# A convolution and mixture-of-experts kernel: the third group's convolution in four pieces a half group on TensorE in place of five

## The chip, the cores and the metric

The kernel runs on one core of one Trainium2 chip. The metric is the device time of one execution in microseconds (us). The kernel before takes 1198.82 us, the median of three runs (1196.96 to 1201.81).

The engines are named as the profile names them: PE is TensorE (PEld its weight loads), DVE is VectorE, ACT is ScalarE, POOL is GpSimd, SP is SyncE, which issues most DMAs.

## The reference

The input `x` has 8 sequences of 2880 positions with 192 channels, so 23040 tokens. Two steps follow each other.

The first is a dynamic convolution: for each token and each of 8 heads, 7 weights come from a softmax over `weight_gen`, and the output is the weighted sum of the token and its 6 predecessors, head by head (24 channels each):

```python
out = np.einsum('bshk,bskhg->bshg', w, x_unf)
```

The second is a two-level mixture of experts. Each token picks the best of 4 groups by `x @ w_group`, then the best of 4 experts in it by `xg @ w_expert[g]`. The expert is `relu(x @ w1) @ w2` with 1024 hidden units, and its output is multiplied by both softmax values:

```python
h = np.maximum(xg[mask_e] @ w1[g, e], 0.0)
ye = h @ w2[g, e]
out[tok_idx] = combined[:, None] * ye
```

## The kernel before

**Groups and half groups.** The 23040 tokens lie on 128 partitions, 180 to a partition. They are worked on in 15 groups of 12 columns (1536 tokens), each in two half groups of 6 columns (`SC = 6`). For a group the kernel loads `xin` and `wt` (`load_group`, L124 and L134, SyncE), takes the softmax (`softmax`, L278 to L292, VectorE with one exponential on ScalarE), convolves (`conv`), scores the tokens against all groups and experts (`logits`: transposes L406 and L407, score matmuls L389, transposes back L433, all on TensorE, with copies L399, L413, L425, L436 on ScalarE), ranks them (`ranks`, L359 to L503, many small VectorE instructions) and scatters each row of tokens to its expert's region in DRAM (`scatter_row`, L516 and L517, GpSimd).

**Two ways to convolve.** A half group needs 7 products of 128 x 1152 elements (L307, VectorE) and their sum. In the first three groups, that is the half groups 0 to 5, TensorE adds: for each piece of a list, VectorE makes the products of the piece, adds those of one piece to each other (L343), and TensorE multiplies the piece by the identity and accumulates it in three banks (L348, three matmuls of 128 x 384 for each piece). After the last piece ScalarE copies the three banks to `xrow` (L351). From the fourth group on VectorE adds all by itself (L325). The lists stand in `SUMS`, one for each half group; `FIVE` is `((0, 1), (2, 3), (4,), (5,), (6,))`: two pairs and three single products, so five pieces, 15 matmuls and two adds. The products use three buffers `pr` in turn.

**Rounds and blocks.** After every group but the first a round of expert blocks can be filled. The first round (after two groups) has ten plain blocks of 128 tokens; the later ones have mostly blocks of 256. A block loads its tokens `xb` from DRAM (L818), its weights (L833 for the first layer of a plain block, L835 and L842 into `raw` for the others, L846 for the second layer), transposes the tokens (L915 for plain blocks, L926 and L927 for the others), and runs the first layer (L953), the relu on ScalarE (L959), the second layer (L991), the scaling by the gate (L1000) and the scatter to the output (L1008, GpSimd).

**What sets the order.** Each engine works through its own instruction list in order. The lists of TensorE, ScalarE, VectorE and SyncE are written out by a planner in the kernel: it keeps an estimated clock for each engine (`clk`, `run`), and `fill` lets the front part (softmax, convolution, scores, ranks) emit VectorE work until its clock reaches that of the expert matmuls. A block may be emitted when its round's tables are due (`arrive`). So a change of one list of pieces shifts the estimated clocks, and with them the places at which later instructions stand, until the order falls back into the old one. The lines that the change acts through, with `1.27` us as the planner's cost of a product or an add and `1.92` as that of a piece on TensorE:

```python
            pieces = sum_banks(CHUNK[g] + n)
            pattern = SUMS[CHUNK[g] + n]
            for j, ks in enumerate(pattern):
```

Of the kernel before, what the change touches and what calls it, by code (L numbers as in the profile page):

```python
# [30 lines left out]
TURNED = ((6, 5), (4,), (3,), (2,), (1,), (0,))  # L31
FOUR = ((0, 1, 2), (3, 4), (5, 6))
FIVE = ((0, 1), (2, 3), (4,), (5,), (6,))
HALF = ((0, 1), (2, 3), (4, 5), (6,))
SUMS = (TURNED, FIVE, FIVE, FIVE, FIVE, FIVE)


class Slot:
# [4 lines left out]
def conv_moe_kernel(ctx: ExitStack, tc: tile.TileContext, x, wgen, w_group, w_expert, w1, w2, out):  # L43
# [254 lines left out]
    def sum_banks(k):  # L298
        at = [(3 * k + i) % 4 for i in range(3)] if k < CHUNK[FIRST] else [2, 0, 1]
        return [banks[a]([P, 2, D]) for a in at]  # L300

    def conv(g, o):
# [3 lines left out]
        def product(c0, k, dst):  # L306
            nc.vector.tensor_tensor(  # L307
                out=dst, in0=o.xin[:, c0 + k:c0 + k + SC, :].rearrange("p s (h g) -> p s h g", g=HG),
                in1=w4[:, c0:c0 + SC, :, k:k + 1].broadcast_to([P, SC, H, HG]), op=ALU.mult)

        for n, c0 in enumerate(range(0, WIDTHS[g], SC)):
            row = o.xrow[n]
            acc = row[:, :, 0:D].rearrange("p s (h g) -> p s h g", g=HG)
            new = lambda: cv.tile([P, SC, H, HG], F32, name="pr", bufs=3)
            if state["slots"] or CHUNK[g] + n >= len(SUMS):
                product(c0, 0, acc)
# [13 lines left out]
# [3 lines that stand above are left out]
# [899 lines left out]
```

## Time and profile before

| What | Value |
|---|---|
| Median of three runs | 1198.82 us |
| Profiled execution | 1198.2 us |
| Its span | 1196.6 us |
| TensorE busy | 1125.1 us, 94% |
| VectorE busy | 955.8 us, 80% |
| ScalarE busy | 643.9 us, 54% |
| GpSimd busy | 583.6 us, 49% |
| DMA traffic | 275.10 MB, mean 230 GB/s |

The profiled execution is one run of the program; its span is the time from its first to its last instruction, and the run's own time is 1.6 us longer. An engine's busy share is an average over the whole span; the third group's convolution, which the change is about, lies in the stretch from about 75 to 120 us, in which the shares are other than on average. In the views, "idle before, releaser" is the time that the engine stood still ahead of a row, and what ended it; "issue" means that nothing which the profile shows was waited for. A matmul of 32-bit floats leaves two records.

### The profile page before, as it was taken

Reading aid. Unit: us, or ns where it says so; the run is one execution under the profiler, and the core shown is the slowest. Engines: PE = TensorE matmul, PEld = TensorE weight load, DVE = VectorE, ACT = ScalarE, POOL = GpSimd, SP = SyncE. Lnnn points to the kernel's source line nnn. Section 1 sums busy time; section 2 is a strip of 40 time slices with the busy share of each in tenths; the row PEclk is TensorE's granted clock in tenths of the full one; section 3 lists DMA queues with packets and bytes.
Section 4 is the critical chain, followed back from the end, with each engine's and each line's share of the span. In section 5 each row is a group of like instructions: output and inputs, shape, how many; then the busy total and the mean of one; then the engine's idle time right before and its main releaser. Section 6 shows DMA issues by size and latency. Waiting matters only on the chain.

```text
span 1196.6 us, 24607 instructions
## 1 busy us (share of the span) xinstructions
PE 1125.1 (94%) x8357; PEld 1062.7 (89%) x8357; DVE 955.8 (80%) x1682; ACT 643.9 (54%) x1235; POOL 583.6 (49%) x613
## 2 busy tenths in 40 slices
PE   5887999999999999999999999999799899999998
PEld 2444888999999999999989999999699899999997
DVE  8899997989998989998988889898374576655661
ACT  1332435555555555565546556565446676555762
POOL 7164284647274745765564738384636312222211
PEclk9898999999999999999999999999999999999999
DMA  5797999887878877778786868767657875655562
GB/s 172 216 312 227 298 310 286 247 272 229 286 233 255 256 249 235 248 246 281 221 284 197 289 202 281 232 181 227 201 154 235 263 241 154 189 174 179 161 200 76
DMA packets 84521, 275.10 MB, mean 230 GB/s; under 512 B 15491, under 2 KB 34379, under 8 KB 82593
## 3 DMA queue, kind: packets, MB, share of 16 engines
q1 hardware_dynamic: 64056, 229.77, 61.3%
q0 software_dynamic: 20208, 43.39, 11.9%
q8 instruction: 67, 1.10, 0.4%
q14 instruction: 70, 0.57, 0.1%
q10 hardware_dynamic: 120, 0.28, 0.1%
HBM read 225.83 MB, written 48.42 MB: 229 GB/s over the span
## 4 chain that ended last, share of the span: by engine, by line
PE 62%; issue 19%; DVE 6%; POOL 4%; ACT 3%; DMA 3%; another core or an unknown queue 2%; POOLq 1%; SPq 0%; DVEq 0%; ACTq 0%
PE py L991 27%; PE ph L953 25%; POOL out L1008 4%; DVE pr L307 2%; PE pl L389 2%; PE ph L348 1%; PE tpx L927 1%; PE tpx L926 1%; DMA xb<-rows 1%; PE tpx L348 1%; PE tp L406 1%; DMA rows<-rem 1%; PE py L348 1%; PE pl L406 1%
## 5 line engine op out<-in xcount | busy, mean ns | idle before, releaser
L953 PE MATMUL ph<-xh,wa 128*128 128x256 f32 (+3 forms) x1992 | 455.5, 303 | 1.2 <-issue 1.1
L1008 POOL DMA_INDIRECT out<-y,xb x189 | 213.9, 1132 | 425.6 <-ACT y L1000 176.7
L991 PE MATMUL py<-wc,hh 128*128 128x192 f32 x2160 | 401.3, 327 | 2.7 <-ACT y L1000 2.2
L953 PE MATMUL ph<-xl,wa 128*128 128x256 f32 (+3 forms) x1328 | 351.9, 286 | 0.3
L991 PEld LDWEIGHTS py<-wc,hh 128*128 128x128 f32 x2160 | 346.0, 190 | 4.7 <-ACT y L1000 2.8
L953 PEld LDWEIGHTS ph<-xh,wa 128*128 128x128 f32 x1992 | 337.7, 190 | 4.2 <-issue 2.1
L959 ACT ACTIVATE hh<-ph 128x512 f32<-128x512 f32 (+2 forms) x296 | 165.9, 561 | 265.9 <-PE ph L953 239.0
L953 PEld LDWEIGHTS ph<-xl,wa 128*128 128x128 f32 x1328 | 252.1, 190 | 1.1 <-issue 0.8
L307 DVE TENSOR_TENSOR pr<-xin,wt 128x1152 f32<-128x1152 f32 x186 | 249.3, 1351 | 4.7 <-PE py L348 3.4
L517 POOL DMA_INDIRECT rows<-xrow,ix x156 | 222.2, 1424 | 45.6 <-POOL ix L516 31.5
L325 DVE TENSOR_TENSOR xrow<-xrow,pr 128x1152 f32<-128x1152 f32 x144 | 194.9, 1353 | 0.7
L883 DVE SCALAR_TENSOR_TENSOR pr<-ph,hh 128x320 fp32r<-128x320 f32 (+2 forms) x128 | 71.7, 560 | 92.5 <-ACT hh L964 85.6
L883 DVE TENSOR_TENSOR wa<-raw,wa 128x1024 fp32r<-128x1024 f32 x83 | 101.3, 1220 | 31.9 <-ACT wa L859 30.7
L516 POOL COPY ix<-posi 128x1 int32<-128x1 int32 x156 | 76.0, 499 | 79.1 <-DMA rows<-xrow,ix 44.7
L993 PE MATMUL py<-wc,hh 128*128 128x384 f32 x352 | 111.6, 364 | 0.0
L964 ACT ACTIVATE hh<-ph 128x320 fp32r<-128x320 f32 (+2 forms) x128 | 63.8, 499 | 72.0 <-PE ph L953 71.1
L994 PE MATMUL py<-wc,pr 128*128 128x192 f32 x352 | 88.5, 251 | 0.0
L859 ACT CAST wa<-raw 128x1024 fp32r<-128x1024 f32 x83 | 87.1, 1050 | 0.0
L868 ACT CAST wa<-raw 128x1024 fp32r<-128x1024 f32 x83 | 86.8, 1046 | 0.0
L1000 ACT ACTIVATE y<-py,xb 128x192 f32<-128x192 f32 x179 | 67.3, 423 | 20.9 <-PE py L991 16.7
L883 DVE TENSOR_TENSOR xl<-tpx,xh 128x512 fp32r<-128x512 f32 (+1 forms) x92 | 59.3, 644 | 11.4 <-ACT xh L933 10.4
L993 PEld LDWEIGHTS py<-wc,hh 128*128 128x128 f32 x352 | 66.5, 189 | 1.3
(194 smaller groups left out, 1355.4 us busy)
## 6 DMA issues: line engine op xcount, KB each, us to landing
wc<-in_moe_w SPq DMA_DIRECT2D x73, 768.0 KB
raw<-in_moe_w SPq DMA_DIRECT2D x83, 512.0 KB
xin<-in_x SPq DMA_DIRECT2D x14, 1728.0 KB
raw<-in_moe_w SPq DMA_DIRECT2D x91, 256.0 KB
raw<-w1lo SPq DMA_DIRECT2D x83, 256.0 KB
raw<-in_moe_w SPq DMA_DIRECT2D x22, 768.0 KB
xb<-rows SPq DMA_DIRECT2D x75, 194.0 KB
wa<-in_moe_w SPq DMA_DIRECT2D x24, 384.0 KB
```

The lines of the kernel that those rows point to most:

```text
L307: nc.vector.tensor_tensor(out=dst, in0=o.xin[:, c0 + k:c0 + k + SC, :].rearrange("p s (h g) -> p s h g", g=HG), in1=w4[:, c0:c0 + SC, :, k ...
L325: nc.vector.tensor_tensor(out=acc, in0=acc, in1=prs[k - 2], op=ALU.add)
L517: written_once(nc.gpsimd.indirect_dma_start(out=rows[:, :], out_offset=bass.IndirectOffsetOnAxis(ap=ix, axis=0), in_=src, in_offset=None, ...
L859: nc.scalar.copy(out=o.wa[:, 0, :], in_=o.raw[0])
L868: nc.scalar.copy(out=o.wa[:, 2, :], in_=o.raw[1])
L883: f(*a, **k)
L953: nc.tensor.matmul(ph[:, v, :], lhsT=w[:, f0:f0 + P], rhs=rhs, start=i == 0, stop=i == len(terms) - 1)
L959: nc.scalar.activation(out=hh, in_=ph, func=AF.Relu)
L991: nc.tensor.matmul(b.acc[t], lhsT=hh[:, v, c], rhs=wc[0][:, f, :], start=f == 0 and not (b.wide and t == 1), stop=f == NFT - 1 and not (b. ...
L993: nc.tensor.matmul(b.py[t], lhsT=hh[:, v, c], rhs=wc[f // 4][:, f % 4].rearrange("p l d -> p (l d)"), start=f == 0, stop=False)
L994: nc.tensor.matmul(b.acc[t], lhsT=hl[:, v, c], rhs=wc[f // 4][:, f % 4, 0, :], start=False, stop=f == NFT - 1)
L1008: ins = nc.gpsimd.indirect_dma_start(out=out[:, :], out_offset=bass.IndirectOffsetOnAxis(ap=b.x.bitcast(I32)[:, t, D + 1:D + 2], axis=0), ...
```

## The change

The half groups 4 and 5, the third group's, take the list `HALF`, which stood in the file without being used:

```diff
 FIVE = ((0, 1), (2, 3), (4,), (5,), (6,))
 HALF = ((0, 1), (2, 3), (4, 5), (6,))
-SUMS = (TURNED, FIVE, FIVE, FIVE, FIVE, FIVE)
+SUMS = (TURNED, FIVE, FIVE, FIVE, HALF, HALF)
```

In each of the two, VectorE adds the products 4 and 5 (one more L343) and TensorE takes them as one piece (three L348 fewer). So 87 L348 matmuls are left of 93, and 13 L343 adds stand where 11 stood. The planner's order moves with it on every engine, up to some 350 us into the program.

VectorE, at the end of half group 4: `pr` are the product buffers, `wt`, `m` and `z` belong to the softmax of the fourth group, which is emitted in between.

```order
 L280 TENSOR_TENSOR wt<-wt,m 128x672
+L343 TENSOR_TENSOR pr<-pr 128x1152
 L307 TENSOR_TENSOR pr<-xin,wt 128x1152
 L286 TENSOR_REDUCE z<-wt 128x96
 L288 TENSOR_SCALAR z<-z 128x96
 L290 RECIPROCAL z<-z 128x96
-L307 TENSOR_TENSOR pr<-xin,wt 128x1152
 L292 TENSOR_TENSOR wt<-wt,z 128x672
-L307 TENSOR_TENSOR pr<-xin,wt 128x1152
+L307 TENSOR_TENSOR pr<-xin,wt 128x1152 x2
 L343 TENSOR_TENSOR pr<-pr 128x1152
```

The new add of products 4 and 5 stands ahead of product 6, and the first product of half group 5 moves behind the softmax's last step.

TensorE, at the end of half group 4: `tpx`, `ph` and `py` are the three banks, `ident` the identity.

```order
 L348 MATMUL ph_694<-pr,ident 128x384
 L348 MATMUL py_695<-pr,ident 128x384
-L348 MATMUL tpx<-pr,ident 128x384
-L348 MATMUL ph_694<-pr,ident 128x384
-L348 MATMUL py_695<-pr,ident 128x384
 L406 MATMUL tp<-ident,xrow 128x128 x2
 L407 MATMUL tp<-ident,rem 128x128
```

One piece of three matmuls is gone ahead of the transposes for the scores.

TensorE, at the end of half group 5, where the first expert blocks begin, before:

```order
L915 MATMUL tp<-ident,xb 96x128 x2
L953 MATMUL ph_984<-xd_180,wa 128x128 x4
L348 MATMUL tpx<-pr,ident 128x384
L348 MATMUL ph_906<-pr,ident 128x384
L348 MATMUL py_907<-pr,ident 128x384
L348 MATMUL tpx<-pr,ident 128x384
L348 MATMUL ph_906<-pr,ident 128x384
L348 MATMUL py_907<-pr,ident 128x384
L953 MATMUL ph_1007<-xd_180,wa 128x128 x4
L915 MATMUL tp<-ident,xb 96x128 x2
L406 MATMUL pl<-ident,xrow 128x128 x2
```

The same place on TensorE now:

```order
L915 MATMUL tp<-ident,xb 96x128 x2
L953 MATMUL ph_979<-xd_180,wa 128x128 x4
L348 MATMUL tpx<-pr,ident 128x384
L348 MATMUL ph_909<-pr,ident 128x384
L348 MATMUL py_910<-pr,ident 128x384
L953 MATMUL ph_992<-xd_180,wa 128x128 x4
L915 MATMUL tp<-ident,xb 96x128 x2
L348 MATMUL tpx<-pr,ident 128x384
L348 MATMUL ph_909<-pr,ident 128x384
L348 MATMUL py_910<-pr,ident 128x384
L953 MATMUL ph_1022<-xd_180,wa 128x128 x4
L991 MATMUL py_1029<-wc,hh 128x192 x2
```

Ahead of the first L915 three pieces of half group 5 stood before, and two stand there now; the expert block's matmuls stand between the last two pieces, and a third L953 and the first L991 come ahead of the score transposes (L406), which follow the last row shown.

## Rows read from the trace of the kernel before

**Rows 1.** The page, part 1: engine busy us (share of the span), instructions.

```profile
PE 1125.1 (94%) x8357; PEld 1062.7 (89%) x8357; DVE 955.8 (80%) x1682; ACT 643.9 (54%) x1235; POOL 583.6 (49%) x613
```

**Rows 2.** Stretches: length, each engine's busy us (instructions), PEclk, DMA share, GB/s.

```profile
90.00:120.00 30.00, 22.02 (x75) 12.73 (x74) 27.85 (x48) 6.47 (x14) 14.40 (x13) 0.89 0.79 228
120.00:150.00 30.00, 28.15 (x254) 26.67 (x252) 28.93 (x67) 12.89 (x35) 7.89 (x9) 1.00 0.92 299
```

**Rows 3.** The chain of waits: start us, us, what.

```profile
112.87 0.65 PE py L348 x2
...
114.19 1.16 PE ph L953 x8
115.35 0.65 PE tpx L348 x2
...
125.03 0.89 PE ph L953 x8
125.93 0.65 PE py L991 x4
```

**Rows 4.** Order of time, VectorE: start us, us, engine, line, out<-in [idle before <-releaser].

```profile
97.61 1.35 DVE L307 TENSOR_TENSOR pr<-xin,wt 128x1152 f32<-128x1152 f32 x1
...
107.97 1.36 DVE L343 TENSOR_TENSOR pr<-pr 128x1152 f32<-128x1152 f32 x1
109.24 3.89 DVE L307 TENSOR_TENSOR pr<-xin,wt 128x1152 f32<-128x1152 f32 x3
113.05 1.35 DVE L307 TENSOR_TENSOR xrow<-xin,wt 128x1152 f32<-128x1152 f32 x1
...
117.33 1.36 DVE L307 TENSOR_TENSOR pr<-xin,wt 128x1152 f32<-128x1152 f32 x1 [1.50 <-PE py L348]
```

**Rows 5.** The chain of waits, TensorE, both half groups.

```profile
96.09 1.65 PE tpx L348 x2
...
102.18 0.65 PE py L348 x2
...
105.45 0.91 PE tpx L348 x2
```

**Rows 6.** Stretches with their granted clock.

```profile
91.00:96.00 5.00, 0.50 (x2) 0.00 (x0) 4.55 (x23) 0.00 (x0) 3.12 (x4) 0.85 0.66 134
96.00:101.00 5.00, 4.91 (x8) 2.79 (x9) 4.90 (x8) 0.76 (x1) 4.08 (x4) 0.50 0.92 299
180.00:185.00 5.00, 5.00 (x28) 5.00 (x27) 1.90 (x5) 0.52 (x3) 0.85 (x1) 0.67 1.04 302
```

**Rows 7.** Order of time: tokens' load on SyncE, first use, score transposes.

```profile
111.11 1.49 SPq L818 DMA_DIRECT2D xb<-rows  x2
...
113.10 0.38 PEld L915 LDWEIGHTS tp<-ident,xb 128*96 128x96 f32 x2 [0.20 <-issue]
...
120.17 0.38 PE L406 MATMUL pl<-ident,xrow 128*128 128x128 f32 x2
```

**Rows 8.** Order of time: late scatter, TensorE's and VectorE's waits, token load.

```profile
172.76 0.98 POOL L517 DMA_INDIRECT rows<-xrow,ix  x1 [0.28 <-POOL ix L516]
...
179.66 1.48 PE L991 MATMUL py<-wc,hh 128*128 128x192 f32 x4 [1.65 <-ACT y L1000]
179.77 0.20 DVE L460 TENSOR_REDUCE smg<-exg 128x12 f32<-128x48 f32 x1 [2.40 <-ACT exg L365]
...
183.11 0.34 SPq L818 DMA_DIRECT2D xb<-rows  x1
...
194.35 0.33 PE L926 MATMUL tpx<-ident,xb 128*128 128x128 f32 x1 [1.14 <-DMA xb<-rows]
```

**Rows 9.** Groups by line, 85 to 120 us: names, count, busy us, mean ns, idle.

```profile
L517 POOL DMA_INDIRECT rows<-xrow,posi x12 | 13.5, 1123 | 13.7 <-DVE units L542 10.3 <-issue 3.4
```

**Rows 10.** Stretches of the late stalls.

```profile
615.00:630.00 15.00, 12.62 (x116) 10.55 (x115) 9.20 (x17) 5.39 (x11) 6.40 (x6) 1.00 0.58 185
855.00:870.00 15.00, 6.74 (x71) 5.63 (x70) 2.22 (x9) 2.55 (x6) 7.56 (x11) 0.77 0.45 151
```

## The prediction

> **What bounds the kernel now.** I read the page's busy table first. TensorE is busy for 94% of the span and VectorE for 80% [rows 1]. The share alone says little, so I read stretches next. Between 120 and 150 us both work almost without a break, and the chain of waits from there on is TensorE's expert matmuls (L953, L991), one after the other. Between 90 and 120 us it is otherwise: VectorE is busy 27.85 of 30 us and TensorE only 22.02, at a granted clock of 0.89 [rows 2]. That is the stretch of the change. There the third group's convolution runs, VectorE makes the products, TensorE adds them up, and TensorE waits for VectorE. So time taken off TensorE here is worth something only where TensorE itself comes last.
>
> **The change part by part.** The two half groups of the third group, c = 4 and c = 5 below, each lose one piece, three matmuls on TensorE, and gain one add of VectorE.
>
> What goes: a matmul of a piece takes 0.65 us on the chain (two records, at 115.35 [rows 3]), so a piece takes 1.95 and two pieces 3.9. That is the naive gain. What comes: products and adds of this size follow each other every 1.27 us (three from 109.24 to 113.05 [rows 4]), so two adds take 2.54. That is the naive loss. Neither is the answer, so I walk both engines through the stretch.
>
> First half group, c = 4. The add of products 4 and 5 takes the place in VectorE's order that product 6 had, at 97.61, so their piece can start at 97.61 + 1.27 = 98.9. Before, product 5 alone went to TensorE at 96.09 and product 6 behind it, and both pieces were done at 102.18 + 0.65 = 102.83 [rows 5]. These 6.74 us are long for two pieces, since the clock was at its lower level, 1.2 GHz (0.50 granted from 96 to 101 [rows 6]), after TensorE had been idle. After the change TensorE has been idle longer still, so I let the same 6.74 us pass: 98.9 + 6.7 = 105.6. This half group ends 2.8 us later although TensorE has a piece less to do. The removed work was hidden in idle time, and the wait for the add takes its place.
>
> Second half group, c = 5. Its first piece stood at 105.45 [rows 5], behind the transposes for the scores of c = 4, which need that sum; it moves by 2.8 to 108.3 and is done at 110.2. (Its data, 1.3 us late, were there before that.) The second piece waits for VectorE, which made its pair at 109.24 [rows 4] and now makes it at 110.5; done at 112.45. Now the order has the first expert block's transposes (L915) and its first matmuls (L953). Their tokens were there at the latest at 113.1: the load was issued at 111.11, and at 113.10 TensorE loaded them as weights for L915 [rows 7], right behind the last piece ahead of it. From the end of that piece (112.87 + 0.65) to the first L953 (114.19) it took 0.67 us, L915 and a copy on ScalarE, and the L953 then 1.16 [rows 3]: 113.1 + 0.67 + 1.16 = 114.95. The pair 4 and 5 is ready at 110.5 + 3 x 1.27 = 114.3, so its piece runs from 114.95 to 116.9. Then 0.89 of L953 and 0.2 of L915 to 118.0. Product 6, ready at 115.6, is no wait; its piece ends at 120.0. Behind it the new order has one more L953 (0.89) and one L991 (0.65, both in [rows 3]) ahead of the score transposes (L406), so these start at 121.5. Before they started at 120.17 [rows 7], with 1.54 us less expert work done. 121.5 - 1.54 = 119.96: a gain of 0.2 us. If the tokens land early enough for L915 at 112.45, the piece is then bound by the pair at 114.3, which is worth 0.65 more: 0.85 at best.
>
> VectorE. Its convolution ends at 113.05 + 2.54 = 115.6 instead of 113.05. Before, it then stood still until 117.33, 1.50 us of it for a product buffer that TensorE was still reading [rows 4]. Now the buffers that it wants first are those of the pair, free at 116.9, and of product 6, free at 120.0. It comes to its third product of the next group at about 121.1 instead of 119.87, so of the 2.54 us half are paid by that wait and 1.2 go on. They make the third group's rows leave 1.2 us later. The last scatter of that group was issued at 172.76, and the load that needs them at 183.11; VectorE itself stood idle 2.40 us at 179.77 for ScalarE [rows 8]. I cost them at nothing. If that cover were gone, TensorE's wait for tokens at 194.35, 1.14 us now [rows 8], would grow by 1.2 us.
>
> The SyncE queue is refilled in another order at four places (the first swaps a weight load and a token load that waits for the second round's rows). The waits that it shortens or lengthens there belong to loads made a block ahead. TensorE's idle time at these places is not for a load, so I take nothing, within 1.2 us either way, the size of the wait for tokens at 194.35 [rows 8], the nearest row in which a load is late.
>
> Scatters of GpSimd run in the first half of the stretch, and the tokens' load, issued at 111.11 [rows 7], waits for the last of them. Twelve of them took 1123 ns on average, and but for the first, which waited for its positions, none waited for a VectorE instruction [rows 9], although VectorE was busy almost all the time; an add stands where a product would stand, so I cost this at nothing. The Trainium skill's page "SBUF — State Buffer", section "SBUF: two separate sides", speaks against it: an op of VectorE with two inputs in SBUF and an op of GpSimd that reads SBUF exclude one another for a whole instruction. By that rule each add could put off the scatters by its whole length, and the sum would be that of the slower rival below. The trace shows no such wait, and the measured row decides for me.
>
> The sum: the profiled execution took 1198.2 us (span 1196.6). 1198.2 - 0.2 = 1198.0. The median of the three runs is 0.6 above the profiled one, so I predict 1198.6.
>
> **Rivals.**
> *Faster.* TensorE is the bound for the rest of the kernel, so what it saves counts: 3.9 us. On top, a stall later on could go, since many instructions up to some 350 us are in another order. At 179.66 TensorE lost 1.65 us to ScalarE [rows 8], and the clock then fell to 0.67 for 5 us [rows 6], a loss of another 5 x 0.33 = 1.65: 3.3 us. Together 1198.8 - 3.9 - 3.3 = 1191.6. For it speaks that TensorE is almost gapless from 120 us; against it that, by the walk above, an add that comes late takes the place of each piece saved.
>
> *Slower: the first block's tokens come late.* Place: L915 now stands ahead of the pair's piece and no longer behind three pieces, so a late load blocks the convolution behind it. If scatters are held by both adds, 2 x 1.36 = 2.7 us [rows 4], TensorE stands still from 112.45 to 116; such a pause at 91 to 96 us was followed by 5 us at half clock [rows 6], 2.5 us lost. 1198.8 + 2.7 + 2.5 = 1204.0. It decides from the point where the load is issued later than about 111.8 (it was 111.11). Against it: the adds come at 97.6 and 113.0, the second after that load was issued, so one of them can hardly hold anything; 1201 is then what is left.
>
> *The late stalls move.* TensorE lost 8.3 of 15 us at 855 to 870 and 2.4 at 615 to 630 [rows 10], both in or right behind the short score matmuls, with no engine that is named as late. Nothing stands in another order there, but TensorE's program is 6 matmuls shorter ahead of it. If one stall goes, 1190.5 to 1196.4; if another of that size comes, 1201 to 1207. For it: other groups' score matmuls, with the same instructions, have no such gap, so it hangs on something fine. Against it: the three runs lie within 4.9 us, so it does not come and go by itself. The Trainium skill's page "Runtime: NRT & Kernel Launch", section "Instruction fetch mechanics", holds that an engine's code is fetched in blocks and that crossing one is mostly hidden; by it a shorter program moves no stall, and this rival falls. No row shows what the stall waits for.
>
> *The change does not do what it says* can't be here: the order has the six matmuls fewer and the two adds more.
>
> **How the numbers follow.** Chances: the forecast (1196 to 1201) 0.62; faster 0.14; slower by late tokens 0.10; late stalls 0.14, half of it on either side. A change is told from none at about 0.5% of this time, 6 us: under 1192.8, or over 1204.8. Of the faster rival a bit under half lies below (0.06), of the late tokens 0.03 above, of the stalls 0.05 below and 0.05 above; I add 0.01 below and 0.02 above for what I have not seen. So faster 0.12, same 0.78, slower 0.10. The range 1192.5 to 1204.5 leaves out about two tenths; the forecast's own, from the best case of the walk (-0.85) to the wait for tokens (+1.2) and the runs' own spread of 2 to 3 us, is 1195.5 to 1201.5.
>
> **What would show it.** Right: c = 4's last piece ends at about 105.6; TensorE idles some 1 us between 112 and 115; the score transposes of c = 5 start near 121.5 with one L991 behind them; VectorE has no wait of over 1 us near 117; and the first tokens that L926 wants come no later than before, measured from the expert matmuls' start. Wrong: a granted clock under 1 between 113 and 120, or L915 later than 113.5 (slower rival); a first expert matmul earlier than 113.3, or no half-clock stretch at 180 (faster rival); or the stretches at 615 and 855 with another busy time of TensorE.

## The result, and the profile after

The changed kernel takes 1207.37 us, the median of seven runs (1201.54 to 1211.03). Beside it the kernel before took 1196.96 us (seven runs, 1191.44 to 1201.81). The ratio is 1.0087, 95% interval [1.0061, 1.0112]: slower by some 10.4 us. 1198.6 us was predicted.

Its profiled execution has a span of 1205.6 us, 9.0 more than before's. Part 1 of its page answers to [rows 1]: busy us (share of the span) and instructions.

```profile
PE 1124.8 (93%) x8345; PEld 1061.6 (88%) x8345; DVE 959.5 (80%) x1684; ACT 645.0 (53%) x1235; POOL 568.7 (47%) x613
```

VectorE has two instructions and 3.7 us more; TensorE has 12 records fewer and is busy for as long as before, in a span 9.0 us longer: what was lost is time in which it stood still, 80.8 us where it was 71.5. The stretches of [rows 2], after the change:

```profile
90.00:120.00 30.00, 16.70 (x63) 10.08 (x63) 29.28 (x51) 5.57 (x13) 13.32 (x13) 0.78 0.78 223
120.00:150.00 30.00, 28.59 (x253) 27.21 (x252) 28.93 (x69) 12.09 (x32) 5.68 (x8) 1.00 0.95 300
```

The stretch of the change looks far worse for TensorE (16.70 us busy where it was 22.02, clock 0.78 where it was 0.89), and yet it isn't where the time went. The third group's pieces, in order of time:

```profile
99.94 1.65 PE L348 MATMUL tpx<-pr,ident 128*128 128x384 f32 x2 [10.78 <-DVE pr L343]
...
104.86 0.81 PE L348 MATMUL py<-pr,ident 128*128 128x384 f32 x2
...
108.07 0.81 PE L348 MATMUL tpx<-pr,ident 128*128 128x384 f32 x2
...
111.77 0.91 PE L348 MATMUL tpx<-pr,ident 128*128 128x384 f32 x2 [1.60 <-DVE pr L343]
...
114.13 0.39 PE L915 MATMUL tp<-ident,xb 128*96 128x128 f32 x2 [0.16 <-DMA xb<-rows]
...
122.51 0.38 PE L406 MATMUL pl<-ident,xrow 128*128 128x128 f32 x2
```

TensorE waits 10.78 us for the new add (before, it stood still for 4.60 us ahead of its piece at 96.09), and the half group is done at 105.67 (104.86 + 0.81). At L915 it waits 0.16 us for tokens. How late the whole runs is best read from a mark that both traces have in the same order: the scaling of each block's output on ScalarE (`y`, L1000). Of its start times, after less before:

| us in the trace of before | 131.5 | 179.2 | 310.0 | 378.0 | 446.1 | 512.9 | 789.6 | 942.3 | 1161.8 |
|---|---|---|---|---|---|---|---|---|---|
| later by, us | 0.77 | 0.29 | 2.31 | 4.88 | 4.54 | 7.77 | 7.17 | 9.02 | 8.87 |

At 91 us, ahead of the change, the new trace was already 0.93 late (the last row of positions, L503, at 92.44 and 91.51). So by 131 us the change has cost nothing (0.77 - 0.93 = -0.16). Then come 2.0 us by 310 us, and three steps behind: 2.6 between 310 and 378 us, 3.2 between 446 and 513, 1.9 between 790 and 942. The orders differ for longer than the some 350 us that I gave: the last row of before that stands elsewhere in the new trace is at 453.8 us on TensorE, 463.0 on VectorE, 450.7 on ScalarE, 475.5 on GpSimd and 368.2 on SyncE. So the first of the three steps lies among the reordered rows, the other two behind most or all of them. The last is made of small pieces: 0.6 at the score burst at 807 us, and the rest mostly between 919 and 942 us, where TensorE waits at L926 for tokens in the new trace (2.26 us at 947.28) but stands still in the old one too (2.14 us in issue at 938.70). The first two lie at a score burst: the 24 matmuls of L389 that score a group, 48 records in some 1.5 us. Before, at 364 us, and after, at 367 us, TensorE and ScalarE in order of time:

```profile
364.43 1.52 PE L389 MATMUL pl<-xT,wr 128*32 128x128 f32 x48
...
366.60 0.48 ACT L425 COPY xT<-pl 128x384 f32<-128x384 f32 x1 [0.70 <-PE pl L389]
```

```profile
366.53 1.50 PE L389 MATMUL pl<-xT,wr 128*32 128x128 f32 x42
368.22 0.38 PE L389 MATMUL pl<-xT,wr 128*32 128x128 f32 x3 [0.19 <-issue]
368.96 0.32 PE L389 MATMUL pl<-xT,wr 128*32 128x128 f32 x2 [0.36 <-issue]
369.70 0.27 PE L389 MATMUL pl<-xT,wr 128*32 128x128 f32 x1 [0.42 <-issue]
...
374.25 0.48 ACT L425 COPY xT<-pl 128x384 f32<-128x384 f32 x1 [6.26 <-remote]
```

After 42 records TensorE goes on in steps of 0.75 us with one to three records each, waiting for nothing that the profile names ("issue"), and ScalarE is released 4 us after the last record. I call this a stalled burst. Nine such bursts lie behind 360 us. In the trace of before six of them are longer than 1.6 us (those at 364, 490 and 807 are not), in that of after all nine. The steps at the three that stall in the new trace alone, 2.6, 3.2 and 0.6 us, make 6.4 of the 9.0 us between the spans.

### The profile page after: what moved, and what is told of

It reads as the page before. It is cut to its first block, busy times and chain, and to the rows that moved or that the text cites. A ratio compares the mean times of both kernels' runs of the same rounds, so it can differ in the third digit from the quotient of the medians.

```text
span 1205.6 us, 24585 instructions
## 1 busy us (share of the span) xinstructions
PE 1124.8 (93%) x8345; PEld 1061.6 (88%) x8345; DVE 959.5 (80%) x1684; ACT 645.0 (53%) x1235; POOL 568.7 (47%) x613
## 4 chain that ended last, share of the span: by engine, by line
PE 64%; issue 19%; DVE 5%; DMA 4%; POOL 4%; another core or an unknown queue 2%; ACT 2%; POOLq 1%; SPq 0%; DVEq 0%; ACTq 0%
PE py L991 28%; PE ph L953 26%; POOL out L1008 4%; DVE pr L307 2%; PE pl L389 2%; DMA xb<-rows 2%; PE tpx L927 1%; PE tpx L926 1%; DMA rows<-xrow,posi 1%; PE ph L348 1%; DMA rows<-rem 1%; PE tp L406 1%; PE pl L406 1%; DMA xin<-in_x 1%
## 5 line engine op out<-in xcount | busy, mean ns | idle before, releaser
L953 PE MATMUL ph<-xh,wa 128*128 128x256 f32 (+3 forms) x1992 | 455.9, 303 | 0.8 <-issue 0.5
L1008 POOL DMA_INDIRECT out<-y,xb x189 | 207.1, 1096 | 446.5 <-ACT y L1000 217.8
L991 PE MATMUL py<-wc,hh 128*128 128x192 f32 x2160 | 401.9, 327 | 1.1 <-ACT y L1000 0.6
L953 PE MATMUL ph<-xl,wa 128*128 128x256 f32 (+3 forms) x1328 | 352.4, 286 | 0.7 <-issue 0.5
L991 PEld LDWEIGHTS py<-wc,hh 128*128 128x128 f32 x2160 | 346.5, 190 | 3.2 <-issue 2.2
L953 PEld LDWEIGHTS ph<-xh,wa 128*128 128x128 f32 x1992 | 337.4, 190 | 5.5 <-issue 3.9
L953 PEld LDWEIGHTS ph<-xl,wa 128*128 128x128 f32 x1328 | 252.0, 190 | 1.6 <-issue 1.5
L516 POOL COPY ix<-posi 128x1 int32<-128x1 int32 x156 | 72.0, 473 | 77.4 <-DMA rows<-xrow,ix 40.9
L1000 ACT ACTIVATE y<-py,xb 128x192 f32<-128x192 f32 x179 | 67.2, 422 | 22.8 <-PE py L991 18.5
```

The source lines that it names most:

```text
L953: nc.tensor.matmul(ph[:, v, :], lhsT=w[:, f0:f0 + P], rhs=rhs, start=i == 0, stop=i == len(terms) - 1)
L991: nc.tensor.matmul(b.acc[t], lhsT=hh[:, v, c], rhs=wc[0][:, f, :], start=f == 0 and not (b.wide and t == 1), stop=f == NFT - 1 and not (b. ...
L1008: ins = nc.gpsimd.indirect_dma_start(out=out[:, :], out_offset=bass.IndirectOffsetOnAxis(ap=b.x.bitcast(I32)[:, t, D + 1:D + 2], axis=0), ...
```

## The experiments

Two things differ between the kernels: the work (two adds, six matmuls) and the order that the planner makes of it. Theory O: the order. (How it would reach the bursts is a guess: later transfers would meet them otherwise.) Theory W: the work. Theory P: the bursts' place in TensorE's program, which is shorter by the six matmuls. Theory L: the density of the burst itself. The kernels that separate them:

**Work and order crossed.** e1 has the work of the change and the planner's charges of before:

```diff
+                if mine and ks == (5,):
+                    nc.vector.tensor_tensor(out=pr, in0=held, in1=pr, op=ALU.add)
...
-                for i, ps in enumerate(pieces):
+                for i, ps in enumerate(pieces if not (mine and ks == (4,)) else []):
```

> The work of the change without its order: at c=4 and 5 of the third group VectorE adds products 4 and 5 and TensorE gets four pieces, but the planner is charged as for five, so that SyncE, ScalarE and GpSimd have the very order of the kernel before, and VectorE and TensorE differ only by the two adds and the six matmuls. Order theory (the loss comes from the new order of loads, tokens and expert work up to 350 us, which the score bursts later meet): no loss, 0.998 to 1.002 of before, and the score bursts stall where before's did (at 429, 616, 681 and 856 us). Work theory (two adds more on VectorE, six matmuls fewer on TensorE cost it directly): 1.007 to 1.010. Position theory (the stalls of the bursts hang on where a burst stands in TensorE's program, here 24 instructions earlier than in before, in after 28 from 350 us on): the bursts stall as in the changed kernel, at 366, 431, 495 us and on, and the time is 1.006 to 1.010.

e2 has the charges of the change and the work of before:

```diff
-                        nc.vector.tensor_tensor(out=pr, in0=pr, in1=p2, op=ALU.add)
+                    if ks == (4, 5):
+                        both = [pr, p2]
...
+                for pr in both if ks == (4, 5) else [pr]:
```

> The order of the changed kernel without its work: the planner is charged as for four pieces and one pair more, but the pair's two products go to TensorE as two pieces, and VectorE doesn't add them. Order theory: the whole loss is here, 1.006 to 1.011 of before, with stalled bursts at 366 and 495 us. Work theory: 0.998 to 1.002. Position theory: TensorE's program is 24 instructions longer than in the changed kernel ahead of the first burst of the main part, within 4 of before's from 350 us on, so bursts stall as in before and the time is 0.998 to 1.003.

e3 and e4 lengthen TensorE's program, e3 in the changed kernel (`ks == (4, 5)`), e4 in the one before (`ks == (4,)`):

```diff
+                    if ks == (4, 5):
+                        for h in range(2):
+                            nc.tensor.matmul(ps[:, h, :], lhsT=ident, rhs=pr[:, 2 * i + h].rearrange("p h g -> p (h g)"), start=False, stop=False)
+                        continue
```

> The changed kernel in order and work, but the three matmuls of the added pair are each cut in two by columns (128x192 and not 128x384), at c=4 and 5: six matmuls, 24 instructions of TensorE, more ahead of the bursts, with the same columns and the same order on every engine. Order theory and work theory: as the changed kernel, 1.006 to 1.011 of before. Position theory: bursts stand within 4 instructions of where before has them from 350 us on, and the time goes back to 0.998 to 1.003.

> The kernel before, with the three matmuls of the piece of product 4 at c=4 and 5 each cut in two by columns: 24 instructions of TensorE more ahead of the bursts, nothing else moved. Order theory and work theory: nothing, 0.998 to 1.002 of before, stalled bursts where before has them. Position theory: other bursts stall than in before, and the time moves by 3 us or more either way, 0.990 to 0.997 or 1.003 to 1.010.

Measured against before: e1 1.0052 [1.0016, 1.0087], e4 1.0016 [0.9979, 1.0053], with the order of before; e2 1.0135 [1.0078, 1.0191], e3 1.0114 [1.0057, 1.0170], with the new one. The four ran side by side on one chip: medians of 1204.22 and 1201.28 us with the old order, 1213.11 and 1209.61 with the new one. The burst at 365 us in e1 and in e2:

```profile
364.72 1.52 PE L392 MATMUL pl<-xT,wr 128*32 128x128 f32 x48
```

```profile
369.39 1.50 PE L393 MATMUL pl<-xT,wr 128*32 128x128 f32 x42
371.18 0.38 PE L393 MATMUL pl<-xT,wr 128*32 128x128 f32 x2 [0.29 <-issue]
```

e4 is clean there like e1, e3 stalled like e2, and so it is at the burst near 490 us. The split follows the order. P is refuted for these two bursts: e3 has the 24 instructions back and stalls all the same, e4 has 24 more and doesn't. W alone doesn't carry it: e2 has none of the work and loses most. But e1 is not free of loss: its interval lies clear of 1, overlaps that of the change, and its 1.0052 lies in none of the three ranges expected (e2's lies above the one of theory O). Its trace is of its fastest execution, 1197.63 us, and so doesn't show where that loss lies.

**The burst thinned out.** Eight score matmuls as soon as their two transposes are copied, in both kernels:

```diff
+            if not early and s2 in (4, 8):
+                score(s2 - 4, xTs[s2 // 2 - 2:s2 // 2])
...
-        for i in range(0, len(xTs), 2):
+        for i in range(0 if early else 4, len(xTs), 2):
```

> The kernel before, with the 24 score matmuls of a half round from the third group on no longer in one burst: eight are issued as soon as their two transposes are copied, so three bursts of eight in place of one of 24; SyncE, VectorE and GpSimd keep their order, ScalarE copies from another bank of PSUM. If the dense burst is what stalls (2 to 4 us lost at each of the 6 to 7 stalled bursts of before), this gains 8 to 20 us: 0.983 to 0.993 of before, and no PE rows of the score matmuls with an idle time ascribed to issue. If the stalls come from elsewhere and only show in the burst, 0.998 to 1.004.

> The same edit in the changed kernel. If the loss of the change lies in more stalled bursts (theory), it ends within 0.2% of s_before_spread, that is 0.983 to 0.994 of before, a gain of 15 to 25 us over the changed kernel. If the loss is in the order of loads as such, it stays 8 to 11 us above s_before_spread.

The gain that theory L expects is missed by both: 1.0035 [1.0008, 1.0062], in the range of its rival, and 1.0083 [1.0055, 1.0112], 0.48% above, where neither branch has it. Theory L is refuted. The stalls come without the dense burst; the longest of s_before_spread:

```profile
873.65 1.06 PE L389 MATMUL pl<-xT,wr 128*32 128x128 f32 x12 [4.73 <-issue]
```

(The edit has a small price of its own: with one bank for all transposes, a pair often waits 0.57 us for ScalarE's copy, eight times between 100 and 1000 us in s_before_spread.)

**One half group alone**, `SUMS` with `HALF` for half group 4 or for 5:

> The change at c=4 alone: three matmuls fewer and one add more; SyncE, ScalarE and GpSimd keep the order of before, VectorE and TensorE differ by 4 and 5 rows. Order theory: 0.998 to 1.002 of before, with clean bursts at 365 and 490 us. Work theory: half the loss, 1.003 to 1.005.

> The change at c=5 alone; SyncE keeps the order of before, the other engines differ by 2 to 20 rows near 110 us. Order theory (the loss needs the reordering on SyncE, which only both half groups together bring): 0.998 to 1.003 of before, with clean bursts at 365 and 490 us. Work theory: half the loss, 1.003 to 1.005.

1.0045 [1.0018, 1.0072] and 1.0026 [0.9998, 1.0055]. Both keep SyncE's order of before, and both have the bursts at 365 and 495 us clean; in h5 TensorE stalls right behind the first of them, 2.85 us in issue at 373 us. So a clean burst is not yet a clean stretch. By its time h4 lies in the range of theory W (1.003 to 1.005) and h5 in that of theory O: with e1 it leaves a loss of up to some 0.5% that goes with the work where bursts stall, and that isn't explained.

**One load on SyncE.** Of the four places at which SyncE's order differs, the last lies at 348 to 368 us. Before, SyncE there:

```profile
352.87 0.33 SPq L835 DMA_DIRECT2D raw<-in_moe_w  x1
...
355.97 0.40 SPq L846 DMA_DIRECT2D wc<-in_moe_w  x1
368.19 0.34 SPq L818 DMA_DIRECT2D xb<-rows  x1
```

And after:

```profile
367.13 0.35 SPq L818 DMA_DIRECT2D xb<-rows  x1
368.19 0.01 SPq L846 DMA_DIRECT2D wc<-in_moe_w  x1
```

The weights of block 26 now stand behind its tokens, which wait for the scatter, and come 12 us later: right behind the burst. That was a tempting cause. x_before puts that one load where the changed kernel has it, x_after where before has it, and nothing else moves:

```diff
+                if a == (26, 0) and upto is None and ready(26) and "t26" not in state:
+                    state["t26"] = True
+                    continue
```

(x_after; x_before never defers block 26.)

> The kernel before with one load moved on SyncE and nothing else on any engine: the third group's main-part block 26 asks for its tokens (xb, which waits for the scatter until about 367 us) ahead of its weights (wc, 768 KB), as the changed kernel has it; before has the weights first, at 356 us. Theory of this one place: the weights come 12 us late, transfers that were done by 366 us fall behind the score burst at 364 us, the burst stalls and 3 us or so are lost by 380 us (time 1.002 to 1.005 of before). Rival (this place is only a symptom): the burst at 364 us stays clean in the trace and the time is 0.998 to 1.002.

> The changed kernel with that one load put back: block 26's weights ahead of its tokens, nothing else moved. Theory of this one place: the burst at 366 us is clean as in before, and 3 us of the changed kernel's loss come back (1.004 to 1.007 of before); the burst at 495 us may follow or not. Rival: still 1.007 to 1.011, with the burst at 366 us stalled.

> The changed kernel unaltered, a second profile of it. If the stalled bursts belong to the program, those at 366, 431 and 495 us stall again, the time is 1.006 to 1.011 of before, and the traces agree within 2 us at 600 us. If they are chance of the single execution, other bursts stall, and the traces differ by 3 us or more by then.

> The kernel before unaltered, a second profile of it. If the stalls belong to the program: bursts at 305, 364 and 490 us clean, those at 429, 616, 681 and 856 us stalled, the span within 2 us of 1196.6. If chance: another pattern.

These four ran on another chip than the experiments above, and there nothing stalled, so that they could not try that cause: before took 1173.55 us (29 runs), x_before 1.0007 [0.9987, 1.0028], x_after 1.0021 [1.0005, 1.0036], the changed kernel 1.0021 [1.0006, 1.0037]. All nine bursts last 1.51 or 1.52 us in all four traces, and no row of TensorE's behind 120 us has an idle time put down to issue. The burst near 615 us of the unaltered kernel before, in its first profile and in before_again:

```profile
615.58 1.50 PE L389 MATMUL pl<-xT,wr 128*32 128x128 f32 x42
617.36 0.38 PE L389 MATMUL pl<-xT,wr 128*32 128x128 f32 x3 [0.28 <-issue]
618.11 0.32 PE L389 MATMUL pl<-xT,wr 128*32 128x128 f32 x2 [0.38 <-issue]
...
624.01 0.55 PE L433 MATMUL pl<-ident,xT 128*128 128x128 f32 x3 [0.92 <-ACT xT L425]
```

```profile
609.71 1.52 PE L389 MATMUL pl<-xT,wr 128*32 128x128 f32 x48
611.16 0.50 PE L953 MATMUL ph<-xh,wa 128*128 128x256 f32 x2
```

The same program, the same instructions. The transfers around it are much alike: stretches of before from 2 us ahead of that burst to 4 us behind its start, then those of before_again (the last three columns are granted clock, DMA share, GB/s):

```profile
613.58:615.58 2.00, 2.00 (x15) 1.77 (x14) 2.00 (x2) 1.29 (x3) 1.69 (x2) 1.00 0.75 259
615.58:617.08 1.50, 1.50 (x43) 1.23 (x43) 1.50 (x3) 1.47 (x3) 0.97 (x1) 1.00 0.30 106
617.08:619.58 2.50, 1.40 (x9) 0.78 (x8) 2.50 (x5) 0.00 (x0) 2.12 (x2) 1.00 0.90 302
```

```profile
607.71:609.71 2.00, 2.00 (x15) 1.77 (x14) 2.00 (x2) 1.29 (x3) 1.68 (x2) 1.00 0.83 308
609.71:611.21 1.50, 1.50 (x50) 1.30 (x49) 1.50 (x3) 1.47 (x3) 0.97 (x1) 1.00 0.48 126
611.21:613.71 2.50, 2.50 (x21) 2.50 (x19) 2.50 (x5) 1.08 (x2) 2.13 (x2) 1.00 0.88 290
```

With a DMA share of 0.90 and of 0.88 behind the burst TensorE is busy 1.40 of 2.50 us in the one and all the time in the other. The fetching of instructions is a rival that was not tested; the page's totals for it are the same in both traces (`q8 instruction: 67, 1.10, 0.4%`: packets, MB, share of the DMA engines).

**Without stalls, and with them.** Six more runs, to see what is left of the change where nothing stalls, and to try block 26 where something does. x3 is the changed kernel with the tokens of blocks 14, 19 and 26 at before's places on SyncE:

```diff
+                if a[1] == 0 and a[0] in (14, 19, 26) and upto is None and ready(a[0]):
+                    state[a] = state.get(a, 0) + 1
+                    if state[a] <= (a[0] != 14):
+                        continue
```

> The changed kernel unaltered, a third time. Two ratios stand so far: 1.0087 where the traces show TensorE stalled in issue at most score bursts of the main part, 1.0021 where they show none. Theory (the change itself costs 2 to 4 us by 310 us, and the rest is what the stalls add to it): with bursts of 1.52 us throughout, 1.001 to 1.004 of before; with bursts of 2 to 4 us, 1.006 to 1.011. Rival (the stalls have nothing to do with it, and the ratio scatters by itself): no relation between the two.

> The changed kernel with SyncE's order of before at the blocks 14, 19 and 26 (tokens and weights in the order of before; only the loads of the next group's inputs at 350 us stay one block earlier), nothing moved on the other engines. If the new load order is what costs the 2 to 4 us that the changed kernel is late by at 310 us: this ends 2 to 4 us ahead of after_third, 0.998 to 1.001 of before without stalls. If the order on TensorE, VectorE and ScalarE does it: within 1.5 us of after_third.

> The work of the change without its order, a second time: the two adds on VectorE and the six matmuls fewer, everything else as in before. Without stalls (bursts of 1.52 us): 0.999 to 1.001. With stalls: 0.999 to 1.008, as they fall.

> The order of the changed kernel with the work of before, a second time. Without stalls: if the order carries the 2 to 4 us, within 1 us of after_third; if the work does, 0.999 to 1.001 of before. With stalls 1.006 to 1.015.

> The kernel before with block 26's tokens asked for ahead of its weights, as the changed kernel has it, a second time: the first time no burst stalled in either kernel, so it could not tell. If bursts stall in this execution: theory of this one place, the burst at 364 us stalls too (2 us or more over 1.52) and the time is 1.002 to 1.006 of before; rival, it stays clean. If none stalls: 0.999 to 1.002 again, and the point stays open.

> The changed kernel with block 26's weights ahead of its tokens, as before has it, a second time. If bursts stall in this execution: theory of this one place, the burst at 367 us is clean and the time is 1.003 to 1.007 of before; rival, it stalls as in the changed kernel and the time is 1.007 to 1.013. If none stalls: 0.999 to 1.003, and the point stays open.

The first four fell on a chip without stalls, the last two on one with them. All results, by chip; "long bursts" are those over 1.6 us of the nine behind 360 us in the kernel's trace:

| kernel | order | where bursts stall: ratio | long bursts | where none stalls: ratio |
|---|---|---|---|---|
| before (medians) | before | 1197.0 to 1200.0 us | 6 | 1173.6 and 1173.2 us |
| e1 | before | 1.0052 | 6 | 1.0004 |
| e4 | before | 1.0016 | 7 | - |
| h4 | before, but for 4 and 5 rows | 1.0045 | 6 | - |
| h5 | before, but for 2 to 20 rows | 1.0026 | 7 | - |
| x_before | before, but for one load | 1.0017 | 5 | 1.0007 |
| after | new | 1.0087 | 9 | 1.0021, 1.0014 |
| e2 | new | 1.0135 | 9 | 1.0007 |
| e3 | new | 1.0114 | 7 | - |
| x_after | new, but for one load | 1.0113 | 9 | 1.0021 |
| x3 | new, but for loads of three blocks | - | - | 0.9986 |

The later intervals are: after_third [0.9992, 1.0036], x3 [0.9970, 1.0003], e1_again [0.9987, 1.0020], e2_again [0.9988, 1.0026], x_before_again [0.9992, 1.0042], x_after_again [1.0077, 1.0149].

Three things follow. The loss of 0.87% was seen only with the stalls: where there are none the change costs 1.6 to 2.5 us (0.14 and 0.21%, the smaller not clear of noise), and all versions lie within 0.25% of before. (None of the chips on record was used on two occasions, so that chip and occasion can't be told apart.) Where there are stalls, four kernels of four with the new order lose more (1.0087 to 1.0135) than any of the five with the old one (1.0016 to 1.0052), and mostly have more long bursts; single intervals overlap. The bursts near 365 and 490 us are the clearest sign: both last over 1.6 us in all four traces with the new order, and neither does in the six with the old one. And block 26's load is a symptom: x_before_again has the bursts at 366 and 493 us clean with the load late, x_after_again stalls with the load early, most of it right behind the first burst:

```profile
372.50 1.95 PE L389 MATMUL pl<-xT,wr 128*32 128x128 f32 x48
...
381.53 0.90 PE L433 MATMUL pl<-ident,xT 128*128 128x128 f32 x3 [3.79 <-issue]
```

x3 came out 3.3 us under after_third beside it by the ratios (0.9986 against 1.0014; the medians are 0.7 us apart), so the load order may carry the small rest; the intervals overlap. But the traces show one piece of it. Near 290 us SyncE asks for a block's tokens ahead of a load of weights before, and behind it after the change, and TensorE waits for them (the first two rows are before's):

```profile
288.44 0.33 SPq L818 DMA_DIRECT2D xb<-rows  x1
289.62 0.33 SPq L835 DMA_DIRECT2D raw<-in_moe_w  x1
```

```profile
287.67 0.33 SPq L835 DMA_DIRECT2D raw<-in_moe_w  x1
...
294.76 0.34 SPq L818 DMA_DIRECT2D xb<-rows  x1
...
297.34 0.33 PE L926 MATMUL tpx<-ident,xb 128*128 128x128 f32 x1 [1.31 <-DMA xb<-rows]
```

That wait is 1.62 us in after_again and 1.42 in after_third, and 0.56 to 1.91 us in the traces of e2, e3 and x_after, while x3 and every kernel with SyncE's order of before have none there (of those with the new one, s_after_spread alone has none). The trace of x3 is 9.3 us longer than that of after_third for another reason: TensorE waits 8.00 us for tokens there at 192.97, ahead of the first load that the edit moves. That wait is 3.29 us in before_again and absent in before, so it scatters with the order unchanged. None of the versions beats the kernel before by what can be told.

**What stays open:** what a stall waits for, why there are none on some chips or occasions, which part of the new order draws more of them, and what e1 and h4 lose.

## Why the prediction was wrong

**What bounds, and the walk: right in its end, lucky at its start.** The whole trace was 0.93 us late before the change, so that is to be taken off each time. The add came as said: its piece started at 99.94, 99.0 without the 0.93, and 98.9 was said. Then the two pieces took 5.73 us (to 105.67), not the 6.74 that I let pass. So half group 4 was done 0.9 us earlier than said, and that 105.67 stands beside the 105.6 of the prediction is luck. It cost nothing, since the next half group then waited for VectorE, which came nearly as said: L915 at 113.20 (113.1 said), the pair's piece at 115.05 (114.95), the score transposes at 121.58 (121.5), all without the 0.93. (As read off the trace L915 stands at 114.13, behind the 113.5 that was named as a sign for the slower rival, but of its wait only 0.16 us were for tokens.) A gain of 0.2 us was said, and 0.16 are measured; from the same row of positions to the same scaling it is 0.34 in after_again and in after_third against before_again. The removed pieces were hidden in idle time, as said; the naive 3.9 us are nowhere.

**VectorE: right.** No wait of over 1 us near 117 us; the third product of the next group started at 122.05, 121.12 without the 0.93, and 121.1 was said. L915 waited 0.16 us for its tokens, so the rival of the late first block fell. Twelve scatters of the stretch took 1032 ns on average, against 1123 [rows 9], with two adds more. The exclusion that the Trainium skill's page "SBUF — State Buffer", section "SBUF: two separate sides", states for an op of VectorE with two inputs in SBUF and a GpSimd op that reads SBUF can't be seen in these rows either.

**SyncE's order: too small, slightly.** It was taken as nothing, within 1.2 us, since TensorE's idle time at these places was not for a load. With the new order it is: 1.31 to 1.62 us at L926 near 297 us in the three traces of the changed kernel, and none in x3. 1.6 to 2.5 us are measured in all where nothing stalls.

**The late stalls: the step that failed.** The sum (1198.2 - 0.2) carried the stalls over as they were, at no cost, and in the traces the three bursts that stall in the changed kernel alone cost 6.4 us. The rival "the late stalls move" was the right case, at 0.14, of which half for the wrong side, and with a price of one stall (1201 to 1207). Three arguments of mine failed. I took the three runs' small spread as a sign that the stalls are fixed; but they came and went with the chip (or the occasion) and with the order, and two other chips showed none. I looked for the cause in the program's length, and e3 and e4 show that the length leaves the bursts at 365 and 490 us as they were. The Trainium skill's page "Runtime: NRT & Kernel Launch", section "Instruction fetch mechanics", has the crossing of a code block as mostly hidden; these two runs don't speak against it. That the rival falls with the length was a wrong step of mine, since the order did what the length didn't. And I weighed one stall coming against one going, as if there were one or two. [Rows 10] showed two stretches, and I didn't count the other bursts: six of nine were stalled already, three could still become so, and in the changed kernel all three did. The steps at 366 us (2.6) and 495 us (3.2) are two of them.

## What to carry to other kernels

Where a profile shows time in "issue" that no engine, wait or transfer accounts for, count all its places before putting a price on a reordering: an edit whose own work comes out at zero still reshuffles hundreds of instructions behind it, and it can land on them. Compare such an edit on more than one chip before believing either sign: the same two kernels gave 1.0087 on one and 1.0014 and 1.0021 on two others. And cross work and order (the new work under the old charges, and the reverse) before explaining a loss by the work.

## What the runs showed of the hardware that was not expected

The unaltered kernel took 1197.0 to 1200.0 us (medians) in four comparisons and 1173.6 and 1173.2 us in two others, on other chips: 2.2% apart with the same program. Of the 26.0 us between the two profiles of before (spans 1196.6 and 1170.6), 21.9 come between 513 and 942 us by the scaling on ScalarE (3.0 and 24.9 us), the stretch with the stalled bursts. Five of these alone, at 551, 616, 681, 747 and 856 us, make 19.6 us (2.7, 4.5, 1.8, 1.5 and 9.1). Where nothing stalls, two kernels run in step from 445 to 850 us to within 0.1 us: after_again stays 2.96 to 3.03 us behind before_again.

A stall can be dearer than its bare idle time: some us at half the clock can follow it. Before, behind the burst at 856 us, the granted clock was 0.50 from 863 to 869 us, and 0.77 on average for 15 us [rows 10]; it fell while TensorE stood still for 6.79 us, up to 866.18; in before_again it is not under 0.95 in any stretch of 2 us from 192 us on. It is not the rule: of the six long bursts of before and the nine of after, one each is followed by such a fall.
